# Linear attention into a GELU MLP: first w_in slice in halves, k decays right behind the scaling of q, all of v through GpSimd's casting queue

## The chip, the cores and the metric

The kernel runs on one core of one Trainium2 chip. The metric is the device time of one launch in microseconds (us), given as the median of several runs. Besides, one execution was profiled; its time and its span (first to last instruction) stand in the table below. The engines are TensorE (PE in the profile, PEld for its weight loads), VectorE (DVE), ScalarE (ACT), GpSimd (POOL) and SyncE (SP, which only issues DMAs here).

## The reference

The input is q, k, v of shape 4 x 8 x 768 x 64 (batch, heads, sequence, head width), float32, with one decay lam per head, and two matrices w_in (512 x 2048) and w_out (2048 x 512). What is computed:

```python
for b in range(nb):                       # blocks of 64 positions
    intra = (qb @ kb.T) * Dmask           # Dmask[i,j] = lam**(i-j) for i >= j, else 0
    out   = intra @ vb + (qb * lam**(pos+1)) @ kv_state
    kv_state = lam**block * kv_state + (kb * lam**(block-1-pos)).T @ vb
x = out as 3072 tokens x 512
result = gelu(x @ w_in) @ w_out           # exact gelu
```

## The kernel before

**Tiling.** The kernel takes blocks of 128 positions: 6 blocks in each of 4 batch entries, 24 chunks in all. Chunk n belongs to batch entry n % 4 and block n // 4. The four chunks of one block make 512 tokens, one group g of the MLP, so there are six groups (0 to 5). All matmuls are in bf16.

**Attention of a chunk.** `scores` (L196) multiplies kT and qT, two heads at a time; DVE applies the decay mask (`sc_m`, L200). `inter` (L223) multiplies the running state with qT; `intra` (L229) adds sc_m times v into the same PSUM bank, and the result is copied into x_t. `next_state` (L208) multiplies `k_dec`, which is k times a decaying power of lam, with v; DVE adds this to the state. `k_dec` is made by `decay_k` (L168): on DVE for chunks 0 to 3, on POOL for the others. The last block (chunks 20 to 23) needs none.

**Transposes.** Chunks 0 to 7 transpose q and k on PE (`transposes`, L175). Chunks 8 to 23 use `dma_transposes` (L183 to L189): SP issues a DMA transpose of k, POOL multiplies q by its power of lam into `q_hat` (L188), and SP issues a DMA transpose of q_hat. `request(n)` calls this for one chunk.

**MLP of a group.** `mlp_blocks(g)` gives a list of blocks of PE work: sixteen of the first matmul (L262, each followed by a GELU on ACT), then the second matmul (L274, L289), whose result ACT copies and SP writes out. In groups 0 and 1 the first four blocks take only three chunks' tokens, and the fourth chunk's follow as one more block.

**Order.** The schedule is written out by hand: every engine does its instructions in program order. `visits` says before which block of which group a piece of attention is issued. From group 1 on two pairs of chunks are worked in each group: `pair_a` (both scores) and, some blocks later, `pair_b` (both inter, both next_state, both intra). In group 1 these are chunks 8, 9 at blocks 10 and 16, and chunks 10, 11 at blocks 21 and 27. `requests(n)` is issued ahead of them: it requests chunks n and n + 1, decays the k of chunks n - 2 and n - 1, and loads chunks n + 2 and n + 3. The first such call is `first_requests`, at block 30 of group 0: it requests chunks 8 and 9, decays chunks 4 to 7, and loads 10 and 11.

**Loads.** q, k and v come in as float32 and are cast to bf16 by the DMA itself, issued from POOL (`load`, L66). POOL's queue at the start is: k0, two iotas, q0 k1 q1 k2 q2 v1 v2 k3 q3, the first of four slices of w_in (L90), v3, the other three, and four slices of w_out (L94). Then follow k, q, v of chunks 4 to 9. v of chunk 0 is the exception: SP loads it as float32 into `v_f` (L73), and ACT casts it (L337). Each of q, k and v has 12 buffers, k_dec, q_hat, kT and qT have 6 each. A DMA issued from POOL waits for the DMA eight before it in that queue.

**The start.** Until the first slice of w_in is there, PE works on chunks 0 to 3 and, in between, on matmuls over a constant tile (`keep_warm`, L324). The first MLP blocks need w_in's columns in order: block 0 columns 0 to 127, block 1 the next 128, and so on. `outputs(live[3])`, which needs v of chunk 3, is issued before block 2.

Of the kernel before, what the change touches and what calls it, by code (L numbers as in the profile page):

```python
# [8 lines left out]
F32 = mybir.dt.float32  # L9
BF16 = mybir.dt.bfloat16  # L10
# [5 lines left out]
def kernel(  # L16
# [10 lines left out]
    nc = tc.nc  # L27

    B, H, S, D = q.shape
    d_model, d_ff = moe_w_in.shape  # L30
# [5 lines left out]
    NK2 = d_ff // 128  # L36
# [3 lines left out]
    M = B  # L40
# [5 lines left out]
    consts = ctx.enter_context(tc.tile_pool(name="consts", bufs=1))  # L46
    w_pool = ctx.enter_context(tc.tile_pool(name="w", bufs=1))
    qkv_pool = ctx.enter_context(tc.tile_pool(name="qkv", bufs=12))
# [8 lines left out]
    raw = {}  # L57
    dram = dict(q=q, k=k, v=v)

    def chunk_of(name, n):  # L60
        b, so = n % B, n // B
        return dram[name][b, :, so * C:(so + 1) * C, :].rearrange("h si d -> si h d")

    def load(n, name):
        raw[n, name] = qkv_pool.tile([128, H, D], BF16, tag=name, name=f"{name}_t")
        nc.gpsimd.dma_start(raw[n, name], chunk_of(name, n))  # L66
# [2 lines left out]
    load(0, "k")  # L69
    lam_b = consts.tile([128, H], F32)  # L70
    nc.sync.dma_start(lam_b, lam[None, :].to_broadcast((128, H)))
    v_f = consts.tile([128, H, D], F32)
    nc.sync.dma_start(v_f, chunk_of("v", 0))  # L73

    pos = consts.tile([128, 1], F32)
    row = consts.tile([128, C], F32)
    nc.gpsimd.iota(pos, pattern=[[0, 1]], base=0, channel_multiplier=1, allow_small_or_imprecise_dtypes=True)
    nc.gpsimd.iota(row, pattern=[[1, C]], base=0, channel_multiplier=0, allow_small_or_imprecise_dtypes=True)
    for item in "q0 k1 q1 k2 q2 v1 v2 k3 q3".split():
        load(int(item[1]), item[0])  # L80

    w_in_t = w_pool.tile([128, NK1, d_ff], BF16)
    w_out_t = w_pool.tile([128, NK2, d_model], BF16)
    w_in_r = moe_w_in.rearrange("(ko ki) f -> ki ko f", ki=128)
    w_out_r = moe_w_out.rearrange("(ko ki) f -> ki ko f", ki=128)
    NS = 4

    def load_w_in(s):
        f = d_ff // NS
        nc.gpsimd.dma_start(w_in_t[:, :, s * f:(s + 1) * f], w_in_r[:, :, s * f:(s + 1) * f])  # L90

    def load_w_out(s):
        f = NK2 // NS
        nc.gpsimd.dma_start(w_out_t[:, s * f:(s + 1) * f, :], w_out_r[:, s * f:(s + 1) * f, :])  # L94

    load_w_in(0)
    load(3, "v")
    for s in range(1, NS):
        load_w_in(s)
    for s in range(NS):  # L100
        load_w_out(s)

# [30 lines left out]
    def late_powers():  # L133
        nc.scalar.activation(lam_c, ln_col, ACT.Exp, scale=float(C))
        nc.scalar.activation(lam_p, ln, ACT.Exp, scale=pos)
# [17 lines left out]
    live = {}  # L153
# [10 lines left out]
    def decay_k(c, eng):  # L164

        if c.so < NB - 1:
            c.k_dec = work_pool.tile([128, H, D], BF16, tag="kd", name="k_dec")
            eng.tensor_mul(c.k_dec, c.k, lam_m[:, :, None].to_broadcast((128, H, D)))  # L168
# [150 lines left out]
    def keep_warm(n, new=True):  # L319

        if new:
            idle_ps[0] = bank([128, 512], F32, "m", "idle_ps")
        for _ in range(n):
            nc.tensor.matmul(idle_ps[0], idle[:, :128], idle, start=True, stop=True)  # L324
# [2 lines left out]
    nc.vector.tensor_mul(dmask, cmask[:, None, :].to_broadcast((128, H, C)),  # L327
                         lam_m[:, :, None].to_broadcast((128, H, C)))
    keep_warm(9)
    raw[0, "v"] = qkv_pool.tile([128, H, D], BF16, tag="v", name="v_t")  # L330
    for n in range(M):
        begin(n)
    transposes(live[0], lambda: keep_warm(3, new=False))
    keep_warm(3, new=False)
    scores(live[0])
    late_powers()
    nc.scalar.copy(live[0].v, v_f)  # L337
    keep_warm(2, new=False)
    transposes(live[1], lambda: keep_warm(1, new=False))
    keep_warm(2)  # L340
# [25 lines left out]
    def request(n):  # L366
        begin(n)
        dma_transposes(live[n])
# [3 lines left out]
    def prefetch(upto):  # L372
        while next_load[0] <= min(upto, NCH - 1):
            for name in "kqv":
                load(next_load[0], name)
            next_load[0] += 1
# [6 lines left out]
    def first_requests():  # L383
        for n in (2 * M, 2 * M + 1):
            request(n)
        for n in range(M, 2 * M):
            decay_k(live[n], nc.gpsimd)
        prefetch(2 * M + 3)


    visits = {
# [6 lines left out]
        (0, 28): [lambda: scores(live[5])],  # L398
        (0, 29): [lambda: transposes(live[6]), lambda: outputs(live[5])],
        (0, 30): [lambda: scores(live[6]), lambda: first_requests()],  # L400
        (0, 31): [lambda: transposes(live[7]), lambda: outputs(live[6])],
        (0, 32): [lambda: scores(live[7])],
# [5 lines left out]
    def pair_a(n):  # L408
        for c in (live[n], live[n + 1]):
            scores(c)  # L410

    def pair_b(n):
        pair = live[n], live[n + 1]
        for c in pair:
            inter(c)
        for c in pair:
            next_state(c)
        for c in pair:
            intra(c)
            take_state(c)  # L420

    def requests(n):
        for m in (n, n + 1):
            request(m)
        for m in (n - 2, n - 1):
            decay_k(live[m], nc.gpsimd)
        prefetch(n + 3)

    def add(g, i, f):
        visits.setdefault((g, i), []).append(f)  # L430


    for g in range(1, NG - 1):
        n = (g + 1) * M
        a0, b0, a1, b1 = (10, 16, 21, 27) if g == 1 else (3, 10, 18, 26)
        add(g, a0 - 2, lambda n=n: requests(n + 2))
        add(g, a0, lambda n=n: pair_a(n))
        add(g, b0, lambda n=n: pair_b(n))
        if g + 2 < NG:
            add(g, b0 + 1, lambda n=n: requests(n + M))  # L440
        else:
            add(g, b0 + 1, lambda n=n: [decay_k(live[m], nc.gpsimd) for m in (n + 2, n + 3)])
        add(g, a1, lambda n=n: pair_a(n + 2))
        add(g, b1, lambda n=n: pair_b(n + 2))

# [36 lines left out]
```

## Time and profile before

| | |
|---|---|
| median of 13 runs | 218.3 us (217.06 to 219.38) |
| profiled execution, time | 218.55 us |
| profiled execution, span | 216.8 us |
| PE busy | 204.7 us (94%), 1429 matmuls |
| POOL busy | 102.3 us (47%) |
| ACT busy / DVE busy | 87.4 us (40%) / 75.8 us (35%) |
| L168 POOL k_dec | 16, 1071 ns each |
| L188 POOL q_hat | 16, 1062 ns each |
| L66 POOL loads of k, q, v | 24, 24 and 23, about 0.9 us each |
| L337 ACT cast of v of chunk 0 | 1, 604 ns |
| DMA of POOL's queue (q0) | 13.51 MB, 84.0% of 16 engines' span |

Times in the profile count from the first instruction. A row of the timeline has start, length, engine, line, operation, output and input, and in brackets the idle time before it with what ended it. A load's POOL time is that of its issue; its landing is given beside it, as the time from issue to landing. A busy PE isn't PE at its peak, but an idle PE is lost time here, since PE is busy for nearly the whole span.

### The profile page before, as it was taken

Reading aid. Unit: us, or ns where it says so; the run is one execution under the profiler, and the core shown is the slowest. Engines: PE = TensorE matmul, PEld = TensorE weight load, DVE = VectorE, ACT = ScalarE, POOL = GpSimd, SP = SyncE. Lnnn points to the kernel's source line nnn. Section 1 sums busy time; section 2 is a strip of 40 time slices with the busy share of each in tenths; the row PEclk is TensorE's granted clock in tenths of the full one; section 3 lists DMA queues with packets and bytes.
Section 4 is the critical chain, followed back from the end, with each engine's and each line's share of the span. In section 5 each row is a group of like instructions: output and inputs, shape, how many; then the busy total and the mean of one; then the engine's idle time right before and its main releaser. Section 6 shows DMA issues by size and latency. Waiting matters only on the chain.

```text
span 216.8 us, 3522 instructions
## 1 busy us (share of the span) xinstructions
PE 204.7 (94%) x1429; PEld 104.7 (48%) x1455; DVE 75.8 (35%) x122; ACT 87.4 (40%) x152; POOL 102.3 (47%) x117
## 2 busy tenths in 40 slices
PE   7987999999997899999999999999999999999993
PEld 2543544455653445445445445445445445444452
DVE  3777220256391745144244245245142222000000
ACT  5663662344655111364511355411365321566121
POOL 7993332883994949677495954960000000000000
PEclk9999999999999999999999999999999999999999
DMA  8999999999899998999979399991340012100112
GB/s 90 137 147 195 206 207 182 172 196 125 170 102 121 75 148 147 166 169 110 111 106 163 64 158 147 108 158 51 106 87 0 3 48 78 67 3 0 48 48 97
DMA packets 100271, 24.48 MB, mean 113 GB/s; under 512 B 92960, under 2 KB 97312, under 8 KB 100256
## 3 DMA queue, kind: packets, MB, share of 16 engines
q0 software_dynamic: 78064, 13.51, 84.0%
q1 hardware_dynamic: 22192, 10.76, 24.9%
q8 instruction: 11, 0.18, 0.4%
q14 instruction: 4, 0.03, 0.1%
HBM read 27.27 MB, written 6.29 MB: 155 GB/s over the span
## 4 chain that ended last, share of the span: by engine, by line
PE 74%; POOL 12%; issue 6%; DMA 6%; ACT 0%; DVE 0%; POOLq 0%
PE h_ps L262 32%; PE o_ps L274 32%; DMA w_in_t<-in_moe_w_in_dram 4%; POOL k_dec L168 3%; POOL k_t L66 3%; PE o_ps L229 2%; POOL q_t L66 2%; DMA q_t<-in_q_dram 2%; PE sc_ps L196 2%; POOL q_hat L188 2%; PE o_ps L289 2%; POOL v_t L66 2%; PE o_ps L223 2%; PE kv_ps L208 1%; PE t_ps L175 1%
## 5 line engine op out<-in xcount | busy, mean ns | idle before, releaser
L262 PE MATMUL h_ps<-x_t,w_in_t 128*128 128x512 bf16 (+2 forms) x404 | 85.7, 362 | 2.1 <-DMA w_in_t<-in_moe_w_in_dram 1.5
L274 PE MATMUL o_ps<-w_out_t,g_t 128*128 128x512 bf16 x356 | 81.7, 379 | 1.0 <-issue 0.6
L264 ACT ACTIVATE g_t<-h_ps 128x512 bf16<-128x512 f32 (+1 forms) x98 | 57.7, 588 | 41.7 <-PE h_ps L262 41.5
L262 PEld LDWEIGHTS <-w_in_t 128*128 128x128 bf16 x416 | 38.4, 98 | 43.5 <-DMA w_in_t<-in_moe_w_in_dram 2.0
L274 PEld LDWEIGHTS <-g_t 128*128 128x128 bf16 x368 | 34.8, 98 | 41.1
L200 DVE TENSOR_TENSOR sc_m<-sc_ps,dmask 128x512 bf16<-128x512 f32 x48 | 30.1, 684 | 37.6 <-PE sc_ps L196 37.6
L279 ACT COPY o_sb<-o_ps 128x512 f32<-128x512 f32 x23 | 13.5, 586 | 70.6 <-PE o_ps L274 67.1
L188 POOL TENSOR_TENSOR q_hat<-q_t,lam_p 128x512 bf16<-128x512 bf16 x16 | 17.0, 1062 | 26.9 <-issue 8.5
L66 POOL DMA_DIRECT2D k_t<-in_k_dram x24 | 22.0, 917 | 6.6 <-DMA w_out_t<-in_moe_w_out_dram 3.1
L66 POOL DMA_DIRECT2D q_t<-in_q_dram x24 | 21.5, 896 | 4.6 <-DMA w_out_t<-in_moe_w_out_dram 2.7
L215 DVE TENSOR_TENSOR tmp<-kv_ps,state 128x512 f32<-128x512 f32 x16 | 11.0, 687 | 33.0 <-PE kv_ps L208 33.0
L66 POOL DMA_DIRECT2D v_t<-in_v_dram x23 | 20.8, 905 | 3.5 <-DMA w_in_t<-in_moe_w_in_dram 1.7
L168 POOL TENSOR_TENSOR k_dec<-k_t,lam_m 128x512 bf16<-128x512 bf16 x16 | 16.8, 1071 | 0.0
L235 DVE CAST x_t<-o_ps 128x512 bf16<-128x512 f32 x16 | 10.3, 683 | 10.2 <-PE o_ps L229 10.2
L216 DVE TENSOR_TENSOR state<-tmp,lam_blk 128x512 bf16<-128x512 f32 x16 | 11.6, 726 | 0.6
L324 PE MATMUL idle_ps<-idle 128*128 128x512 bf16 x29 | 10.2, 460 | 1.2 <-DVE idle L104 1.2
L181 DVE TENSOR_TENSOR qT<-t_ps,lam_q 128x512 bf16<-128x512 bf16 x8 | 5.5, 692 | 14.0 <-PE t_ps L175 13.6
L208 PE MATMUL kv_ps<-v_t,k_dec 128*128 128x128 bf16 x80 | 6.5, 219 | 2.9 <-POOL k_dec L168 2.9
L196 PEld LDWEIGHTS <-kT 64*128 64x128 bf16 x192 | 5.7, 94 | 6.5 <-issue 4.0
L196 PE MATMUL sc_ps<-qT,kT 64*128 64x128 bf16 x192 | 8.2, 217 | 0.6 <-DVE qT L181 0.2
L229 PE MATMUL o_ps<-sc_m,v_t 128*64 128x128 bf16 x192 | 8.6, 223 | 0.1
L180 ACT COPY kT<-t_ps 128x512 bf16<-128x512 bf16 x8 | 4.7, 584 | 7.0 <-PE t_ps L175 7.0
(41 smaller groups left out, 72.1 us busy)
## 6 DMA issues: line engine op xcount, KB each, us to landing
out_dram<-o_sb SPq DMA_DIRECT2D x23, 256.0 KB, 2.3
k_t<-in_k_dram POOLq DMA_DIRECT2D x24, 128.0 KB, 4.6
q_t<-in_q_dram POOLq DMA_DIRECT2D x24, 128.0 KB, 5.9
v_t<-in_v_dram POOLq DMA_DIRECT2D x23, 128.0 KB, 5.9
w_in_t<-in_moe_w_in_dram POOLq DMA_DIRECT2D x4, 512.0 KB, 10.7
w_out_t<-in_moe_w_out_dram POOLq DMA_DIRECT2D x4, 512.0 KB, 18.0
v_f<-in_v_dram SPq DMA_DIRECT2D x1, 256.0 KB, 3.5
kT<-k_t SPq DMA_TRANSPOSE x16, 4.8
```

The costliest lines, as they stand in the source:

```text
L66: nc.gpsimd.dma_start(raw[n, name], chunk_of(name, n))
L168: eng.tensor_mul(c.k_dec, c.k, lam_m[:, :, None].to_broadcast((128, H, D)))
L188: nc.gpsimd.tensor_mul(q_hat, c.q, lam_p[:, :, None].to_broadcast((128, H, D)))
L196: nc.tensor.matmul(sc_ps[hi][:, hp, :], c.kT[p, hp, :], c.qT[p, hp, :], start=True, stop=True)
L200: nc.vector.tensor_mul(c.sc_m[:, :, hi, :], sc_ps[hi], dmask_r[:, :, hi, :])
L215: nc.vector.tensor_add(tmp, kv_ps, states[c.b])
L216: nc.vector.tensor_mul(new, tmp, lam_blk)
L229: nc.tensor.matmul(c.o_ps[hi * D:(hi + 1) * D, hp, :], c.v[:, 2 * hp + hi, :], c.sc_m[:, hp, hi, :], start=(c.so == 0 and hp == 0), stop=T ...
L262: nc.tensor.matmul(h_ps[:, f, :], w, x_t[:, ki, lo:hi], start=(ki == 0 and f == 0), stop=(ki == NK1 - 1), skip_group_check=True)
L264: nc.scalar.activation(g_t[:, kf:kf + n_kf, lo:hi], h_ps, ACT.Gelu)
L274: nc.tensor.matmul(om[io], g_t[:, kf, io * C:(io + 1) * C], w_out_t[:, kf, :], start=(kf == 0), stop=(kf == NK2 - 1))
L279: nc.scalar.copy(o_sb, om[io])
```

## The change

Three edits. The cast of v of chunk 0 goes: its load is issued by POOL like the others, between q1 and k2. The first slice of w_in, 512 columns, is loaded by two DMAs of 256 columns; v of chunk 3 follows both. `requests(n)` decays the k of its own chunks n and n + 1, behind their q_hat, instead of those of n - 2 and n - 1; chunks 8 and 9 are decayed at the end of `first_requests`, behind the loads of chunks 10 and 11, and the separate call for chunks 18 and 19 falls away. The number of decays is the same.

```diff
-    v_f = consts.tile([128, H, D], F32)
-    nc.sync.dma_start(v_f, chunk_of("v", 0))
...
-    for item in "q0 k1 q1 k2 q2 v1 v2 k3 q3".split():
+    for item in "q0 k1 q1 v0 k2 q2 v1 v2 k3 q3".split():
...
-    def load_w_in(s):
-        f = d_ff // NS
-        nc.gpsimd.dma_start(w_in_t[:, :, s * f:(s + 1) * f], w_in_r[:, :, s * f:(s + 1) * f])
+    def load_w_in(lo, hi):
+        f = slice(lo * 128, hi * 128)
+        nc.gpsimd.dma_start(w_in_t[:, :, f], w_in_r[:, :, f])
...
-    load_w_in(0)
+    load_w_in(0, 2)
+    load_w_in(2, 4)
     load(3, "v")
-    for s in range(1, NS):
-        load_w_in(s)
+    for s in range(4, NK2, 4):
+        load_w_in(s, s + 4)
...
-    raw[0, "v"] = qkv_pool.tile([128, H, D], BF16, tag="v", name="v_t")
...
-    nc.scalar.copy(live[0].v, v_f)
...
     def first_requests():
...
         prefetch(2 * M + 3)
+        for n in (2 * M, 2 * M + 1):
+            decay_k(live[n], nc.gpsimd)
...
     def requests(n):
         for m in (n, n + 1):
             request(m)
-        for m in (n - 2, n - 1):
+        for m in (n, n + 1):
             decay_k(live[m], nc.gpsimd)
         prefetch(n + 3)
...
         if g + 2 < NG:
             add(g, b0 + 1, lambda n=n: requests(n + M))
-        else:
-            add(g, b0 + 1, lambda n=n: [decay_k(live[m], nc.gpsimd) for m in (n + 2, n + 3)])
```

## The prediction

> **What bounds the kernel now.** I read the page first: TensorE (PE) is busy 94% of the span and its clock is granted in full in every slice, so only PE's idle time is to be had, plus whatever the change adds in front of PE. The chain that ended last goes through PE for most of the span, but 12% of it through GpSimd (POOL):
>
> ```profile
> PE 74%; POOL 12%; issue 6%; DMA 6%; ACT 0%; DVE 0%; POOLq 0%
> ```
>
> Next the list of waits. Of the waits in which PE stands, these are the large ones (columns: waited for, us in total, times, longest):
>
> ```profile
> PE kv_ps L208 <- POOL k_dec L168: 2.9, 3, 1.8
> PE h_ps L262 <- DMA w_in_t<-in_moe_w_in_dram: 1.5, 1, 1.5
> ```
>
> The timeline of PE shows where the first of them lies. A pair of chunks is finished by `pair_b`: eight matmuls of L223, eight of L208, sixteen of L229.
>
> ```profile
> 68.36 0.61 PE L223 MATMUL o_ps<-qT,state 128*128 128x128 bf16 x8
> 70.78 0.40 PE L208 MATMUL kv_ps<-v_t,k_dec 128*128 128x128 bf16 x4 [1.82 <-POOL k_dec L168]
> 71.78 0.40 PE L208 MATMUL kv_ps<-v_t,k_dec 128*128 128x128 bf16 x4 [0.60 <-POOL k_dec L168]
> ...
> 82.85 0.61 PE L223 MATMUL o_ps<-qT,state 128*128 128x128 bf16 x8
> ...
> 84.17 0.40 PE L208 MATMUL kv_ps<-v_t,k_dec 128*128 128x128 bf16 x4 [0.49 <-POOL k_dec L168]
> ```
>
> The next L262 or L274 block starts at 72.68 and 85.07, so these two visits last 4.32 and 2.22 us. The undisturbed ones (99.55 to 101.11) last 1.56. The loss is 2.76 + 0.66 = **3.42 us**, a little over the 2.9 us of idle time, since a pipeline that stops must also refill. From 85 us to the end no PE wait of any size is left.
>
> Why k_dec is late is in the timeline of POOL:
>
> ```profile
> 54.95 4.04 POOL L168 TENSOR_TENSOR k_dec<-k_t,lam_m 128x512 bf16<-128x512 bf16 x4
> 58.94 0.95 POOL L66 DMA_DIRECT2D k_t<-in_k_dram  x1
> ...
> 64.45 1.04 POOL L188 TENSOR_TENSOR q_hat<-q_t,lam_p 128x512 bf16<-128x512 bf16 x1 [0.19 <-DMA q_t<-in_q_dram]
> 68.69 1.04 POOL L188 TENSOR_TENSOR q_hat<-q_t,lam_p 128x512 bf16<-128x512 bf16 x1 [3.19 <-DMA q_t<-in_q_dram]
> 69.69 2.04 POOL L168 TENSOR_TENSOR k_dec<-k_t,lam_m 128x512 bf16<-128x512 bf16 x2
> ```
>
> POOL issues the loads of chunks 10 and 11 (58.94 to 64.27), then stands in q_hat of 10 and of 11 until those same loads land, and only then decays k of 8 and 9, whose k landed long before. PE waits behind a transfer that it doesn't need yet.
>
> The second place is the start. Loads go out one per 0.87 us and land about 4.3 us after issue. w_in's first slice is issued at 10.51 and lands 8.0 us later, at 18.51; PE's last warming matmul ends at 17.04.
>
> ```profile
> 18.56 1.47 PE L262 MATMUL h_ps<-x_t,w_in_t 128*128 128x384 bf16 x8 [1.52 <-DMA w_in_t<-in_moe_w_in_dram]
> 19.96 0.41 PE L229 MATMUL o_ps<-sc_m,v_t 128*64 128x128 bf16 x8
> ```
>
> **What the Trainium skill says.** (1) Perfetto Trace Analysis, DMA Instruction — SWDGE: the profiled end of a GpSimd DMA is the end of descriptor generation, not of the data. The trace agrees: 0.88 us on POOL, 4.3 us to landing. (2) DMA: Bandwidth & Descriptors, Issuing engines are not separate DMA queues: DMAs from SP and GpSimd run on the same 16 engines and interleave. So moving v of chunk 0 to GpSimd takes no bytes away. The trace shows a difference in time only: v_f was issued by SP at 1.20 and landed 3.5 us later, mostly before the first k load landed at 5.35. (3) The same page, Specifications: a transfer wants runs of at least 512 B. Half a w_in slice has rows of 256 bf16, just that; no transfer with such rows is in this trace.
>
> **The change part by part.** Numbers are against the profiled execution: span 216.8, time 218.55, which is 0.25 above the median of the 13 runs, 218.3.
>
> (a) k decays behind q_hat. The count stays: 16 POOL decays of 1.04 us. In POOL's order k_dec of 8 and 9 moves ahead of q_hat of 10 and 11, directly behind the loads of 10 and 11, and every later pair moves two chunks forward. k_dec 8 and 9 would start near 64.3 and end at 66.4, against PE's need at 68.9. k_dec 10 and 11 then take the old place, 69.7 to 71.7, against PE's need at 83.3. Both stalls go: **-3.42 us**.
> What is moved past: q_hat 10 is pushed from 64.45 to about 66.4, and with it on SP's queue the DMA transpose of its q, the kT transpose of 11 and the qT transpose of 11. q_hat 11 waits for its load until 68.7 in any case, so qT 11, which was issued at 69.75 and landed 2.4 us later at 72.15, moves by the shift of (b) and some tenths at most. Its reader is `pair_a` at 77.10, which comes to about 74.7. There is 1 to 2 us of cover. The decay also needs a free one of six k_dec buffers, that of the chunk six earlier: chunk 4's was read at 57.3, and later ones are read at least ten us ahead. The loads of 12 and 13, behind the decays, start at 71.7 as before.
>
> (b) v of chunk 0 through POOL. Removed: one SP issue (0.41), one cast on ACT (0.60, at 7.20, with ACT idle for 1.11 us after it). Added: one POOL issue of 0.87 ahead of k2, q2, v1, v2, k3, q3 and everything later, and 128 KB more in that queue. It lands at the place of k2 now, 9.5, and PE wants v at 9.68: nothing, 0.2 at most. But k2 to q3 land 0.87 later, and PE did wait for q2 (10.5) and q3 (14.48). So the warm-up ends near 17.9 instead of 17.04. The stream from this queue doesn't drain until after 50 us (POOL waits for earlier transfers before most issues from 18.8 to 38), so its delay carries on to the loads of chunks 4 to 9. Bounds: 0.5 (v_f no longer shares the engines with the first load) to 0.9; I take 0.8.
>
> (c) The first slice in halves. One more POOL issue (0.75 to 0.83, hidden: the engines are some 3 us behind POOL there). q3 landed at 14.45, the slice 4.06 later. A half should take 1.7 to 2.3: it lands at 17.2 to 17.7, the other near 19.3, v of chunk 3 near 20.2. So the first w_in matmul starts at 17.9, PE itself now being last: 0.65 us earlier. This isn't kept. Before, v3 landed at 19.36 for L229 at 19.96 (0.6 us of cover), slice 1 at 21.8 for a need near 22.6 (0.8), and k_dec 5 was ready at 57.05 for 57.52 (0.5), being behind q_hat 9 whose load landed at 53.9. Their covers are all shorter than the delay. Whole slices land 2.4 us apart later (24.6, 27.0), so two halves cost 2.4 to 3 us, up to 0.6 more than one whole; I take 0.1. Queue delay: 0.8 + 0.1 = 0.9, minus the smallest cover, 0.5: PE is **+0.4 us** late at 57.5 (bounds: -0.1 and +0.9), and (a)'s times move by 0.9, with k_dec 9 ready at 67.3 and still ahead of PE.
>
> Sum: -3.42 + 0.4 = -3.0: 215.5 for the profiled execution, 215.3 against the median. **The forecast is 215.3 us**, with 214.8 to 215.9 from the bounds of (b) and (c).
>
> **The rivals.**
> R1, the transposes become late (chance 0.10). With the decays ahead of q_hat 10, four transposes on SP run closer together, beside the loads; kT 10 took 6.3 us and qT 10 4.0 in such company. If qT 11 slips by 3 us to about 75.2 plus the 0.9, `pair_a` at 74.7 waits 1.4; a worse slip gives up to 2. Against it: qT 11 itself took 2.4. Time: 216.6 to 217.3.
> R2, the early queue decides (chance 0.07), and ends on the other side. If each half row costs an engine what a whole row does, the first slice takes 4.06 more instead of 0.1; the delay is 0.8 + 4.1 = 4.9, PE is 4.9 - 0.5 = 4.4 late at 57.5, and 3.42 are given back: +1.0, 219.3. It decides from a queue delay of 3.9 on (3.42 + 0.5). For it: this row size is nowhere in the trace. Against it: the 256 B rows of q, k and v move in 0.87 us per 1024, so an engine isn't bound to a fixed price near that of a long row.
> R3, the order isn't what holds k_dec back (chance 0.06): the decays wait for a buffer or the stall moves whole to the next pair. Then only +0.4 is left: 218.7, no measurable change. Against it: chunk 2's buffer was read by 28.7, and k8 landed at 50.8.
>
> **How the numbers follow.** The main case has 0.77, R1 0.10, R2 0.07, R3 0.06. A measurement of this kernel tells about 0.3% (0.65 us) from no change, so faster means below 217.65. Main and R1 lie there: 0.87. R3 gives 0.06 of no change; R2 is split, 0.01 to no change and 0.06 to slower. The range runs from 214.5, where all of the start's 0.65 is kept on top of the 3.42 to within a few tenths, to 217.3, R1's end. Left out are R2, R3 and some 0.05 below and above.
>
> **What would show it.** In the profile after, "PE kv_ps <- POOL k_dec" at 68 to 84 us is gone and the visits there last 1.56 us; in POOL's timeline a pair of decays stands between the loads of 11 and q_hat of 10, before 67.5. The first L262 starts near 17.9, a short wait for v3, slice 1 or k_dec 5 follows, and v_f and its cast are gone. Wrong would be: a wait of sc_ps for qT at the second pair (R1), first half and second half landing over 3 us apart (R2), decays early but kv_ps still waiting (R3), or a first matmul before 17.5 with nothing late behind it, which would make me too cautious by 0.5 to 1 us.

## The result, and the profile after

The kernel with the three edits takes **215.84 us** (median of 11 runs, 214.69 to 216.4) against 218.36 for the kernel before (48 runs, 216.52 to 221.4): 2.5 us less, a ratio of 0.9885 with a 95% interval of 0.986 to 0.991. The forecast was 215.3 with a range of 214.5 to 217.3. The profiled execution took 216.26 us with a span of 214.5, so it is 0.4 above its median; the one before was 0.2 above its own. Of 71 executions of the kernel before that ran beside the experiments, 27 had a mean granted TensorE clock of 0.989 to 0.992 (median 219.0 us) and 44 one of 0.997 to 1.000, called full clock below (217.6), while all 11 of the kernel after had full clock.

The chain that ended last, from the page of the kernel after. POOL's share has gone from 12% to 5%, PE's from 74% to 87%, and no k_dec is in it any more:

```profile
PE 87%; POOL 5%; DMA 4%; issue 1%; DVE 0%; ACT 0%; POOLq 0%
```

The timeline of PE after, at the two `pair_b` visits (the lines are numbered one or two lower, as the file is shorter):

```profile
69.42 0.61 PE L222 MATMUL o_ps<-qT,state 128*128 128x128 bf16 x8
69.87 0.61 PE L207 MATMUL kv_ps<-v_t,k_dec 128*128 128x128 bf16 x8
70.41 0.64 PE L228 MATMUL o_ps<-sc_m,v_t 128*64 128x128 bf16 x16
70.98 1.04 PE L261 MATMUL h_ps<-x_t,w_in_t 128*128 128x512 bf16 x3
...
81.14 0.61 PE L222 MATMUL o_ps<-qT,state 128*128 128x128 bf16 x8
81.59 0.61 PE L207 MATMUL kv_ps<-v_t,k_dec 128*128 128x128 bf16 x8
82.13 0.64 PE L228 MATMUL o_ps<-sc_m,v_t 128*64 128x128 bf16 x16
82.70 5.35 PE L273 MATMUL o_ps<-w_out_t,g_t 128*128 128x512 bf16 x23
```

There is no bracket behind kv_ps, and each visit lasts 1.56 us (69.42 to 70.98, 81.14 to 82.70). Before they lasted 4.32 and 2.22. The cause is in POOL's timeline after:

```profile
64.13 0.92 POOL L66 DMA_DIRECT2D v_t<-in_v_dram  x1
65.02 2.09 POOL L167 TENSOR_TENSOR k_dec<-k_t,lam_m 128x512 bf16<-128x512 bf16 x2
67.03 1.08 POOL L187 TENSOR_TENSOR q_hat<-q_t,lam_p 128x512 bf16<-128x512 bf16 x1
69.70 1.04 POOL L187 TENSOR_TENSOR q_hat<-q_t,lam_p 128x512 bf16<-128x512 bf16 x1 [1.59 <-DMA q_t<-in_q_dram]
70.71 2.49 POOL L167 TENSOR_TENSOR k_dec<-k_t,lam_m 128x512 bf16<-128x512 bf16 x2
```

The decays of chunks 8 and 9 stand between the last load and q_hat of 10, and are done at 67.1, 2.8 us before PE asks. POOL still waits for the load of q 11, but nobody waits for POOL meanwhile.

The start went the other way. PE after, from 14 us on:

```profile
16.45 0.40 PE L174 MATMUL t_ps<-ident,q_t 128*128 128x128 bf16 x4 [1.43 <-DMA q_t<-in_q_dram]
...
18.83 1.46 PE L261 MATMUL h_ps<-x_t,w_in_t 128*128 128x384 bf16 x8
21.03 0.41 PE L228 MATMUL o_ps<-sc_m,v_t 128*64 128x128 bf16 x8 [0.74 <-DMA v_t<-in_v_dram]
```

q of chunk 3 landed at 16.41 (14.45 before), the first half at 17.78, the second at 20.7, v of chunk 3 at 20.96 (19.36 before). The output matmuls of chunk 3 begin at 21.03 instead of 19.96. From there to the first pair PE keeps this distance: kv_ps of chunks 4 and 5 at 58.37 against 57.30, the first `pair_b` at 69.42 against 68.36. So in the two profiles: +1.07 at the start, -2.76 and -0.66 at the two visits, -2.35 in sum; the spans differ by 2.3.

### The profile page after: what moved, and what is told of

It reads as the page before. It is cut to its first block, busy times and chain, and to the rows that moved or that the text cites. A ratio compares the mean times of both kernels' runs of the same rounds, so it can differ in the third digit from the quotient of the medians.

```text
span 214.5 us, 3520 instructions
## 1 busy us (share of the span) xinstructions
PE 204.7 (95%) x1429; PEld 105.2 (49%) x1455; DVE 78.2 (36%) x122; ACT 87.0 (41%) x151; POOL 104.2 (49%) x119
## 2 busy tenths in 40 slices
DMA packets 100799, 24.35 MB, mean 114 GB/s; under 512 B 92976, under 2 KB 97840, under 8 KB 100784
## 4 chain that ended last, share of the span: by engine, by line
PE 87%; POOL 5%; DMA 4%; issue 1%; DVE 0%; ACT 0%; POOLq 0%
PE h_ps L261 38%; PE o_ps L273 37%; DMA v_t<-in_v_dram 4%; PE o_ps L228 3%; PE sc_ps L195 3%; PE kv_ps L207 2%; PE o_ps L222 2%; POOL k_t L66 2%; PE o_ps L288 2%; POOL q_t L66 2%; POOL v_t L66 1%; PE t_ps L174 1%; POOL w_in_t L88 1%; DVE qT L180 0%; ACT o_sb L292 0%
## 5 line engine op out<-in xcount | busy, mean ns | idle before, releaser
L66 POOL DMA_DIRECT2D v_t<-in_v_dram x24 | 21.7, 907 | 4.0 <-DMA w_out_t<-in_moe_w_out_dram 1.6
L215 DVE TENSOR_TENSOR state<-tmp,lam_blk 128x512 bf16<-128x512 f32 x16 | 13.5, 846 | 0.6
L323 PE MATMUL idle_ps<-idle 128*128 128x512 bf16 x29 | 10.9, 486 | 1.2 <-DVE idle L103 1.2
L228 PEld LDWEIGHTS <-v_t 128*64 128x64 bf16 x192 | 5.9, 109 | 3.5 <-DMA v_t<-in_v_dram 1.6
```

What stands on the lines that cost most here:

```text
L215: nc.vector.tensor_mul(new, tmp, lam_blk)
L228: nc.tensor.matmul(c.o_ps[hi * D:(hi + 1) * D, hp, :], c.v[:, 2 * hp + hi, :], c.sc_m[:, hp, hi, :], start=(c.so == 0 and hp == 0), stop=T ...
```

## The experiments

The kernels are built from the kernel before, by the three edits one at a time and in two of the three pairs (v of chunk 0 with the halves, without the decays, wasn't run), and by changes to the load order. Each has its median, and its ratio to the kernel before on the same chip with its interval. Numbers 1 to 4, 5 to 8 and 9 to 12 ran on three different chips, so a difference of medians across these groups is less sure than one within a group. A single profiled execution can lie 1.5 us off its kernel's median here, so small differences are read from medians only.

**1. The decays alone** (e1). Edit: the last three hunks of the change's diff, nothing else.

> Only the k decays are moved; v of chunk 0 still comes through SP and ACT, the first w_in slice is whole. Theory A (the decays give 3.42 us and the two load edits together cost about 1.1): both pair_b visits last 1.56 us, the kv_ps of chunks 4 and 5 stays at 57.3, span 213.4, time 214.9 to 215.1, about 0.8 faster than with all three edits. Theory B (the load edits are neutral and the decays alone give only the 2.5 that was measured, since something else takes up the rest): 215.8, as with all three edits.

Measured: 214.96 us, ratio 0.9857 (0.9827 to 0.9886), span 213.2; kv_ps of chunks 4 and 5 at 57.13, both visits undisturbed. Theory A. By the medians the decays alone give 3.4 us, as much as the sum of the two stalls, and are 0.9 better than all three edits together. Among runs at full clock the difference is 2.5 us: 214.93 (5 runs) against 217.44 (25).

**2. v of chunk 0 alone** (e2). Edit: `v_f` and its cast out, `v0` behind `q1` in the list of loads.

> Only v of chunk 0 goes through GpSimd's queue. Theory A1 (the extra load makes the late start): q of chunk 3 lands near 16.4 instead of 14.45, the output matmuls of chunk 3 come near 20.9 instead of 19.96, and kv_ps of chunks 4 and 5 is 0.8 to 1.1 late. POOL's chain to k_dec of 8 and 9 is 0.8 late too, so the time is 0.8 to 1.0 longer: 219.2. Theory A2 (the halves make it): q of chunk 3 lands 0.9 later, at 15.3, and the output matmuls of chunk 3 come at about 20.3; 218.6.

Measured: 219.02 us, ratio 1.0044 (1.0019 to 1.0068): slower by 0.65, between the two (at full clock by 1.3: 218.70 against 217.44). The profiled execution was the fastest of its 22 (217.49), so its landings (q of chunk 3 at 15.31, v of chunk 3 at 19.02) tell of the delay to q 3, 0.86, but not of the median. The stalls at k_dec still stand in it, but they are smaller than in the profile before:

```profile
69.69 0.40 PE L206 MATMUL kv_ps<-v_t,k_dec 128*128 128x128 bf16 x4 [0.59 <-POOL k_dec L166]
70.69 0.40 PE L206 MATMUL kv_ps<-v_t,k_dec 128*128 128x128 bf16 x4 [0.60 <-POOL k_dec L166]
...
83.01 0.40 PE L206 MATMUL kv_ps<-v_t,k_dec 128*128 128x128 bf16 x4 [0.43 <-POOL k_dec L166]
```

The two visits last 3.09 and 2.16 us here, a loss of 2.13 and not of 3.42, since q of chunk 11 landed at 67.5 and not at 68.6.

**3. The halves alone** (e3). Edit:

```diff
...
-    load_w_in(0)
+    load_w_in(0, 2)
+    load_w_in(2, 4)
     load(3, "v")
...
```

> Only the first w_in slice is loaded in halves. Theory A1: the first half lands near 17, the first w_in matmul starts at 17.1 to 17.3, v of chunk 3 lands at 19.4 to 19.6 so that its matmuls stay near 19.9, and nothing is gained or lost at the end: 218.1 to 218.4. Theory A2: v of chunk 3 lands 0.8 to 1.0 later than before, near 20.3, and the time is up to 0.5 longer: 218.8.

Measured: 217.79 us, ratio 0.9977 (0.9951 to 1.0003). A small gain or none; neither theory had a gain, and at full clock there is none (217.56 against 217.44). PE's first w_in matmul started at 16.84:

```profile
16.84 1.46 PE L263 MATMUL h_ps<-x_t,w_in_t 128*128 128x384 bf16 x8
18.23 0.41 PE L230 MATMUL o_ps<-sc_m,v_t 128*64 128x128 bf16 x8
```

The slice's first half landed at 15.59 here and v of chunk 3 at 17.87, so PE was 1.7 ahead of the kernel before at this point, and still 1.2 ahead at the first `pair_b` (67.13 against 68.36): in this execution the early start was kept up to there. That execution (217.26) is 0.5 faster than its median, and the stalls at k_dec still stand behind it (visits of 4.04 and 2.41 us, a loss of 3.33).

**4. Decays and halves, v of chunk 0 as before** (e4).

> The decays moved and the first slice in halves; v of chunk 0 as before, through SP and ACT. Theory A1 (v of chunk 0 in the casting queue makes the late start): as with the decays alone, 214.8 to 215.1, kv_ps of 4 and 5 at 57.1 to 57.4. Theory A2 (the halves make it): 215.5 to 215.9, kv_ps of 4 and 5 near 58.

Measured: 214.78 us, ratio 0.9862 (0.9824 to 0.99): as theory A1 has it. In PE's timeline of this kernel:

```profile
16.72 1.46 PE L263 MATMUL h_ps<-x_t,w_in_t 128*128 128x384 bf16 x8
20.11 0.41 PE L230 MATMUL o_ps<-sc_m,v_t 128*64 128x128 bf16 x8 [1.93 <-DVE lam_blk L142]
```

The first matmul is 1.84 earlier than in the kernel before, and then PE stands 1.93 us. The releaser named is not the cause: L230 doesn't read lam_blk, and v of chunk 3, which it reads, landed at 20.07. So in this execution what the first half brings forward is lost at a load queued behind the second half.

**5. Decays and v of chunk 0, the slice whole** (e5).

> The decays moved and v of chunk 0 through GpSimd's queue; the first w_in slice whole. Theory C1 (v of chunk 0 costs its queue delay wherever it is put): about 1.0 above the decays alone, 215.9 to 216.1, as with all three edits. Theory C2 (its delay shows only together with the halves, since with a whole slice PE waits for the slice anyway): 215.0 to 215.4.

Measured: 216.29 us, ratio 0.9895 (0.9856 to 0.9934). Theory C1, and a little more: 1.3 above the decays alone by the medians, 0.8 by the ratios, and all six runs lie above the five of the decays alone at full clock. The cost doesn't need the halves.

**6. All three, v of chunk 3 between the halves** (e6), and **7. the same with v of chunk 0 as before** (e7). Edit for both:

```diff
     load_w_in(0, 2)
-    load_w_in(2, 4)
     load(3, "v")
+    load_w_in(2, 4)
```

> All three edits, but v of chunk 3 is loaded between the two halves of the slice and not behind both. Theory D1 (PE's wait at the output matmuls of chunk 3 is for its place in the queue): v of chunk 3 lands about 1.3 earlier, near 19.6, the output matmuls of chunk 3 come 0.7 earlier, 215.0 to 215.3. Theory D2 (the second half or the next slice is then what is late): the wait moves to the third w_in block or to slice 1, 215.7 to 215.9.

> Decays moved, halves with v of chunk 3 between them, and v of chunk 0 as before through SP and ACT. Theory D1: the first w_in matmul at 16.7, the wait of 1.9 at the output matmuls of chunk 3 falls to under 0.8, kv_ps of chunks 4 and 5 is 0.5 to 1.0 earlier than with the decays and halves alone if the decays of 4 and 5 let it, 214.0 to 214.5. Theory D2: 214.8, no change.

Measured: 215.26 us, ratio 0.9853 (0.9813 to 0.9892), against 215.84 in the old order: in D1's direction, though the intervals overlap. v of chunk 3 landed at 18.60 and its matmuls came at 20.25, with no wait. Number 7: 214.61 us, ratio 0.9809 (0.9767 to 0.985), against 214.78: 0.2 less by the medians, 1.2 by the ratios, and the intervals overlap, so it stays open. In its profile the wait is 0.61, at the third w_in block, which reads the second half (landed at 20.21), so there the wait moved as D2 has it.

**8. Only the decays of chunks 8 and 9 moved** (e8). Edit:

```diff
+        for n in (2 * M, 2 * M + 1):
+            decay_k(live[n], nc.gpsimd)
...
-        for m in (n - 2, n - 1):
+        for m in (n - 2, n - 1) if n > 2 * M + 2 else ():
```

> Only the decays of chunks 8 and 9 are moved to the end of first_requests; all later pairs keep their place, two chunks behind. Theory E1 (a pair's wait is its own): the visit of chunks 8 and 9 is 2.76 shorter, the next one still loses 0.66, 215.6. Theory E2 (the second pair's decays stay behind q_hat of 13 at 82, so PE, now earlier, stands there for what it gained): the visit of chunks 10 and 11 lasts 4.5 to 5 us instead of 2.22, and the time is 217.9 to 218.4.

Measured: 215.7 us, ratio 0.9887 (0.9834 to 0.9939), span 213.3. The time is E1's, the reason is neither's. POOL and PE of this kernel:

```profile
77.56 1.04 POOL L188 TENSOR_TENSOR q_hat<-q_t,lam_p 128x512 bf16<-128x512 bf16 x1 [1.52 <-DMA q_t<-in_q_dram]
78.56 2.04 POOL L168 TENSOR_TENSOR k_dec<-k_t,lam_m 128x512 bf16<-128x512 bf16 x2
```

```profile
79.97 0.61 PE L223 MATMUL o_ps<-qT,state 128*128 128x128 bf16 x8
80.42 0.64 PE L208 MATMUL kv_ps<-v_t,k_dec 128*128 128x128 bf16 x8
```

With two decays fewer in front, the loads of chunks 12 and 13 went out earlier and q 13 was there at 77.5 instead of 81; the decays of 10 and 11 ended at 80.6, just when PE asks. Both stalls are gone with one pair moved, in this execution with no cover left. That the median is 0.7 above number 1 could be this missing cover in other executions; this wasn't shown.

**9 and 10. One and two spare loads at the place of v of chunk 0** (e9, e10), on number 4.

```diff
-    for item in "q0 k1 q1 k2 q2 v1 v2 k3 q3".split():
+    for item in "q0 k1 q1 s0 s1 k2 q2 v1 v2 k3 q3".split():
...
```

Number 9 has `s0` only. An item `s` loads v of chunk 0 once more, into a tile of its own.

> Decays moved, halves, v of chunk 0 through SP and ACT as before, and besides one spare load of the same 128 KB by GpSimd at the place where the change puts v of chunk 0; nothing reads it. Theory F1 (the place in GpSimd's queue is the whole cost): as with all three edits, 215.7 to 216.0, 1.0 to 1.2 above decays and halves alone. Theory F2 (taking the transfer off SP gives some of it back): 216.1 to 216.4. Theory F3 (it isn't the queue, but that v of chunk 0 itself comes late): 214.8, no cost.

> As the last, with two spare loads there. F1: another 0.9 to 1.2, 216.7 to 217.0. F3: 214.8. If the early delay had cover that the first spare load uses up, the second costs more than the first.

Measured: 215.17 us, ratio 0.9875 (0.9829 to 0.9921), and 216.25, ratio 0.9911 (0.9881 to 0.9941). F3 falls with number 10: two loads that nobody reads cost 1.5 us there (1.1 by the ratios), and all its runs lie above five of the six of number 4. F1 is right in kind, but by the medians the first costs 0.4, within the intervals, and the second 1.1. That fits some cover, as the last sentence of the second expectation has it, but the intervals don't tell the first from the second; a place in the queue costs 0.74 on average of the two. F2, that removing the SP transfer gives something back, has no support: all three edits (215.84) are above one spare load, not below it; the intervals overlap.

**11 and 12. The output matmuls of chunk 3 one w_in block later** (e11 on number 4, e12 on all three edits).

```diff
-        (0, 2): [lambda: outputs(live[3])],
+        (0, 3): [lambda: outputs(live[3])],
```

> Decays moved, halves, v of chunk 0 as before; the output matmuls of chunk 3 are issued before the fourth w_in block instead of before the third, so v of chunk 3 may come 0.65 later. Theory G1 (that load is the deadline that eats the early first matmul): 214.2 to 214.5. Theory G2 (the next deadline, slice 1 or the decays of 4 and 5, stands at the same time): 214.8.

> All three edits, and the output matmuls of chunk 3 one w_in block later. G1: the wait of 0.74 there falls to about 0.1, 215.2 to 215.4. G2: 215.8, with the wait moved to slice 1 or to kv_ps of chunks 4 and 5.

Measured: 214.40 us, ratio 0.9827 (0.9787 to 0.9868), and 215.54, ratio 0.9888 (0.9843 to 0.9933). Each is some 0.3 to 0.4 below its partner by the medians, in or near G1's range, but inside the intervals, and by the ratios number 12 gains nothing (0.9888 against 0.9885): not settled. The profile of number 12, which loads in the same order as the kernel after, shows how much one execution differs from another:

```profile
15.30 0.40 PE L174 MATMUL t_ps<-ident,q_t 128*128 128x128 bf16 x4
...
17.69 2.11 PE L261 MATMUL h_ps<-x_t,w_in_t 128*128 128x384 bf16 x12
19.73 0.41 PE L228 MATMUL o_ps<-sc_m,v_t 128*64 128x128 bf16 x8
```

q of chunk 3 landed at 15.29 here and at 16.41 in the profile of the kernel after, v of chunk 3 at 19.13 and at 20.96, with nothing before them changed. Number 11 has the late q of chunk 3 without the second edit:

```profile
16.00 0.40 PE L176 MATMUL t_ps<-ident,q_t 128*128 128x128 bf16 x4 [1.32 <-DMA q_t<-in_q_dram]
```

**What the edits are worth**, from the medians. The decays: 218.37 to 214.96 is -3.4 (with the halves -3.0, with v of chunk 0 -2.7). v of chunk 0 through POOL, in five pairs that differ by it alone: +0.65 by itself, +1.33 on the decays, +1.06 on decays and halves, +0.65 with v of chunk 3 between, +1.14 with the later output matmuls; +0.97 on average, always a loss (by the ratios 0.5 to 1.3, on average 0.9). The halves: -0.58, -0.18 on the decays, -0.45 on decays and v of chunk 0; none of these is clear of its interval, and by the ratios they are -0.5, +0.1 and -0.2, so a gain isn't shown. The averages of the three edits, -3.05 + 0.97 - 0.40, make the measured -2.5, which is no check of its own, as the same medians stand on both sides.

**The clock has a part in these medians.** The lower clock was seen in 46 of 115 runs of the kernels in which k_dec of chunks 8 and 9 comes late (before, 2 and 3), and in 7 of 78 of all the others (on the chip of numbers 9 to 12 alone 3 of 17 against 4 of 30). So the moved decays probably also make the longer executions rarer. At full clock they are worth 2.5 alone, 2.8 with the halves and 2.4 with v of chunk 0, and the kernel after is 1.7 faster than the kernel before (215.84 against the 217.57 of the 44 runs, which weren't made beside it). Whether the stalls bring the lower clock isn't shown: none of the profiles here has it.

The versions with the decays and without the second edit have lower medians than both kernels: numbers 1, 4, 7 and 11 lie between 214.4 and 215.0, and their intervals don't tell them apart.

## Why the prediction was right

**The decays (step a): right in kind; the close match in size is partly luck.** The sum of 3.42 us was taken from the length of the visits in one profile, and alone the edit gives 3.41 by the medians. But the stalls differ between executions: where they still stand, the visits lost 2.13 us in the profile of number 2 and 3.33 in that of number 3. At full clock the edit is worth 2.5; the rest of the 3.41 goes with the lower clock, which 18 of 43 runs of the kernel before had on that chip and one of six of number 1, and of which the prediction knew nothing. k_dec 8 and 9 were forecast to end at 67.3 with the queue delay, and ended at 67.1. q_hat of 10 was pushed to 67.03, and `pair_a` of 10 and 11 at 75.40 showed no wait, so R1 fell. R3 fell with number 1.

**v of chunk 0 (step b): right in kind, about the upper bound in size.** The forecast took 0.8 of queue delay and an end effect of 0.4 for both load edits, 0.9 at most. The medians give 0.97 for this edit and 0.88 (215.84 against 214.96) for both. Two terms were mis-sized. First the delay: in the profile after, v of chunk 3 landed 1.60 later than before, not 0.9, since q of chunk 3, taken as 0.87 late, was 1.96 late. Number 12 shows that about 1 us of that belongs to the execution; number 2 had 0.86. Numbers 7 and 11 have a late q of chunk 3 without this edit (PE waited for it until 15.44 and 16.00). All profiles with this extra delay load in halves, but others with halves don't have it, so a part of the halves in it is open. Second the reference itself: covers of 0.5 to 0.8 us were read from one execution, when landings vary by about as much. Such a cover can't be counted on as a whole in the median. By the medians of numbers 9 and 10 it is about half a place in the queue, which their intervals don't fix.

**The halves (step c): right in the sum; the start was put wrong in the profile after.** The first matmul was put at 17.9 instead of 18.56 and came at 18.83; in number 12, at 17.69. That the early start "isn't kept", because v of chunk 3 follows at once, is what number 4 shows (16.72, then 1.93 us of wait); in number 3 it was kept up to the first stall. A half was put at 1.7 to 2.3 us behind q of chunk 3, but in six of the nine profiles with halves, the one after among them, it landed 1.3 to 1.4 behind. The step priced the halves at a loss of 0.1; the medians lean to a gain of 0.2 to 0.6, which isn't clear of the intervals. Of the three places that the step named as the end of the cover, v of chunk 3 was the one that decided in the profile after: its wait of 0.74 is there, while k_dec of chunk 5 was ready at 57.8 for a need at 58.6. By then the delay of the queue had shrunk from 1.6 to 0.8 (q_hat of 9 at 54.73 against 53.95).

**R2** asked whether half rows cost as much as whole ones. They don't: in the DMA records of the profile after, a packet of half a row (512 B written) took 60 ns in the median and one of a whole row (1024 B) 98, and number 3 is not slower than the kernel before. The sign named for R2, halves over 3 us apart, was nearly there in the profile after (2.9) without R2 being so: in number 3 they landed 1.4 apart.

**Two slips of the working.** The bounds -0.1 and +0.9 on 218.3 - 3.42 give 214.8 to 215.8, not 215.9. And moving v of chunk 0 does take some bytes away, 24.35 MB on the page after against 24.48, since its float32 copy is no longer written. Neither changes the forecast.

## What to carry to other kernels

On an engine that works in program order, put what depends on old data ahead of what depends on the transfer that was just issued; the price of the wrong order is read from the longer visits of the engine that waits, refill included, and in more than one execution. A load added to a full casting queue is paid by everything behind it, even if its own bytes only moved from another queue. When a first piece is made to land earlier, look at once for the next load that the same engine needs, since the gain can end there, as in number 4.

## What was not expected of the hardware

The same list of transfers lands up to 1.8 us apart from one execution to the next: v of chunk 3 at 19.13 and 20.96 in two kernels with the same queue, q of chunk 3 at 15.29 and 16.41. A pause of some 1.2 to 1.6 us in the stream falls on another transfer from profile to profile: inside the first slice in the kernel before (4.06 us for it, where later slices land 2.5 apart), at q of chunk 3 and again at the second half in the profile after, at v of chunk 3 in numbers 4 and 5, while number 3 has hardly any up to there. What makes it isn't shown.

The mean granted clock of an execution was either 0.997 to 1.000 or 0.982 to 0.992, with nothing between, and for the kernel before the lower one took 1.4 us more. With the stalls at k_dec still in, runs spread over 216.5 to 221.4; with the decays alone five of six lay between 214.65 and 215.22, and the sixth, at 218.63, was the one with a clock of 0.992.
